# Value columns in another order, so that a unit of the attention's output and each output weight piece are one load

## The chip, the cores and the metric

One core of one Trainium2 chip runs the whole program. The metric is device time in microseconds (us), the median of several executions. Engines: PE is the matmul engine (PEld its weight loads), DVE the vector engine, ACT the scalar engine, POOL is GpSimd, and SP issues nearly all DMAs. A core has 16 DMA engines, which share the packets of a DMA between them.

## The reference

The input x has 2048 tokens of 640 values. The core of what is computed:

```python
xn  = layernorm(x)
q, k, v = split(xn @ wqkv)             # 32 heads of 20 values
s   = q @ k.T * 20 ** -0.5, only where 0 <= i - j < 256
a   = (softmax(s) @ v).reshape(2048, 640) @ wo
g   = silu(relu(xn @ w1 + b1) ** 2 @ w2 + b2)    # 1536 hidden values
out = x + a * g
```

## The kernel before, in words

All matmuls run on values split into a high and a low part, three products (high by high, high by low, low by high) for each, so a sum over 640 inputs takes 5 chunks x 3 = 15 matmuls.

**Start (L138 to L410).** x is loaded, normalised and transposed; the first q and k columns and all values are computed. The value weights come as five pieces `wvr` of 128 x 640 (L293). `wjobs` (L294) holds a triple of high, low and raw for each, and `split_w` (L187 to L189) works through it: ACT copies the high part, POOL subtracts for the low one. `v_part` (L231 to L233) multiplies with both. The order of the 640 columns in the pieces is the order in which values lie from there on: in v, in the attention's output and in the rows of `wo` that belong to it.

**Main part.** 16 pairs of heads by 16 tiles of 128 tokens are worked through in steps: scores, softmax, probabilities times values (L561, `ops`). PE's time between these is filled by a generator, `filler()`, with q and k groups for later pairs and the MLP (`hps`, `yps`, L473). A planner's clock, which counts estimated costs of PE's work, decides when each piece of work of another engine is written into the program: `later(wait, fn)` (L597) puts a task off until the clock has moved by `wait`. Engines and queues then work strictly in the order in which the program was written. Weights come through `piece` and `piece_pair` (L795 to L827): one load into one of three raw buffers `wraw`, a high part by ACT, a low part by DVE.

**The attention's output.** For a pair of heads and a group of 4 tiles, ACT copies `ops` into `osb` and SP stores it to `o_d[g]` (L568, issued at L588), in DRAM, as 128 rows of 256 tokens. Row 64h + 32e + d holds value d (0 to 19) of head h of the pair and tile parity e; row 20 holds the softmax's sum.

**The last stage.** It has 8 units u of 256 tokens, two for each of the four stores' groups g.
- `invert` (L1074 to L1087) loads a group's 64 rows of sums twice (L1081, `rec<-o`), after a planned wait FETCH takes the reciprocal on DVE (L1084) and stores it (L1085).
- `load(u)` (L1117 to L1131) brings a unit into `ob`: partition 32k + head, 5 chunks c of 256 tokens, where chunk c of block k is value 4c + k. These are four DMAs of 32 x 5 x 256 (L1126). A fifth, `sums` (L1127), reads the unit's 32 rows of reciprocals four times, once for each block k. For unit 0 alone, the planned wait BRING puts off what follows.
- `turn_out` (L1135 to L1151): DVE multiplies ob by sums in two cuts (L1145), ACT makes the high part `oT` (L1146), DVE the low one (L1149).
- `queue_wo` (L1161 to L1170) queues five output weight pieces of 128 rows, row 32k + head of piece c being the row of wo for value 4c + k of that head: four DMAs of 32 x 640 each (L1169, L798 to L801).
- `out_filler` (L1172 to L1218): for each unit 2 tiles x 2 halves of 15 matmuls (`wops`, L627), evacuation by DVE (L1209), the addition of x on POOL (L1215), a store of the tile. Around them it issues the loads of x (`xres`, L1115), of the MLP's results (`yq`, `yk`, L1104), and the next units.

`late()` (L933) calls load(0), load(1) and load(2) during the last groups of the MLP, whose evacuation on DVE is L1013 (`ysb`, from the bank `yps` and the earlier half `yin`). SP's DMAs use eight semaphores in turn, so that a DMA isn't issued before the one eight ahead of it has landed.

Of the kernel before, what the change touches and what calls it, by code (L numbers as in the profile page):

```python
# [19 lines left out]
H = 32  # L20
DH = 20
# [5 lines left out]
VW = DH + 1  # L27
# [22 lines left out]
SETTLE = 0.45  # L50
LEAD = 0.15
FETCH = 8.0
BRING = 8.0
SOON = 0.25
PATIENCE = 0.5

# [1 line left out]
def f32(ap):  # L58
    return ap.bitcast(F32)
# [3 lines left out]
def attn_mlp_kernel(ctx: ExitStack, tc, x, wqkv, wo, w1, b1, w2, b2, out):  # L63
    nc = tc.nc
# [25 lines left out]
    o_d = [dram.tile([NP, P, MT], F32, name=f"o_{g}") for g in range(NB)]  # L90
# [47 lines left out]
    with tc.tile_pool(name="ph1v", bufs=2) as p1v, tc.tile_pool(name="ph1", bufs=2) as p1, tc.tile_pool(name="ph1x", bufs=4) as p1b, tc.tile_pool(name="ph1w", bufs=1) as p1w, tc.tile_pool(name="ph1t", bufs=2, space=PSUM) as p1t:  # L138
# [9 lines left out]
        wv = [p1w.tile([P, KC, D], F32R, name=f"wv{p}") for p in range(2)]  # L148
# [119 lines left out]
        with tc.manual_schedule(engines={E_.PE, E_.Activation, E_.DVE, E_.Pool, E_.SP}):  # L268
# [15 lines left out]
            wjobs = []  # L284
# [6 lines left out]
            wvr = [wvt[c // 3][:, c % 3 * D:(c % 3 + 1) * D] for c in range(KC)]  # L291
            for c in range(KC):
                nc.sync.dma_start(wvr[c], wqkv[c * P:(c + 1) * P, 2 * D:3 * D])  # L293
                wjobs.append((wv[0][:, c, :], wv[1][:, c, :], wvr[c]))  # L294

            def root(t):
                nc.scalar.activation(rstd[:, t:t + 1], mv[:, t, 1:2], AF.Sqrt, bias=eps)
# [195 lines left out]
    def max_rows(p, g, tps):  # L493
        i = p % 2

        def one(j):
            r = slice(j * HP, (j + 1) * HP)
            nc.tensor.transpose(tps[:HP, j, 3 * P:3 * P + HP], mts[g % 2][r, :], ident[r, r])
        both(lambda: one(0), lambda: one(1), COST[P])

        def rest():
            row = at2.tile([8, P], F32, tag="row", bufs=1, name="row")
            mrow = at2.tile([8, 2, P], F32R, tag="mrow", bufs=1, name="mrow")
            nc.scalar.activation(row.rearrange("m (j n) -> m j n", j=2), tps[:8, :, 3 * P:3 * P + HP], AF.Copy, scale=-1.0)  # L504
            nc.scalar.activation(mrow[:, 0, :], row, AF.Copy)
            nc.gpsimd.tensor_sub(mrow[:, 1, :], row, f32(mrow[:, 0, :]))
            for a in range(2):
                nc.sync.dma_start(f32(qs[i])[KR + a:KR + a + HP + 1:HP, g * BT:(g + 1) * BT].rearrange("h (q n) -> h q n", q=4), f32(mrow)[:, a, :])
        return rest
# [3 lines left out]
    def pair_tile():  # L513
        return ptp.tile([P, 2, BT], F32, tag="st", name="stps")
# [25 lines left out]
    def burst_at(p, kb):  # L540
        return next((ts for ts in bursts(p) if ts[-1] == kb), None)
# [57 lines left out]
    def later(wait, fn):  # L599
        tasks.append((clock[0] + wait, len(tasks), fn))  # L600
# [177 lines left out]
    def subtract(tag, jobs):  # L778
        left = [len(jobs)]

        def put_off(k, job):
            def go():
                if item in lows:
                    lows.remove(item)
                    job()
                    left[0] -= 1
                    if not left[0]:
                        held[0] -= 1
            item = (tag, go)
            lows.append(item)  # L790
            later(1.9 + 0.7 * k, go)
        for k, job in enumerate(jobs):
            put_off(k, job)

    def piece(tag, src, go):  # L795
        def start():
            raw = wgt.tile([P, FHALF], F32, tag="wraw", bufs=RAW, name="raw")[:, :RAWN[tag[0]]]
            if isinstance(src, list):  # L798
                for k, rows in enumerate(src):
                    nc.sync.dma_start(raw[32 * k:32 * k + H], rows)  # L800
                return lambda tag: go(tag, raw)  # L801
            if len(src.shape) == 3:
                raw = raw.rearrange("p (c n) -> p c n", n=src.shape[-1])
            nc.sync.dma_start(raw, src)
            return lambda tag: go(tag, raw)
        queue.append((tag, start))
# [16 lines left out]
    def piece_pair(tag, hi, lo, src):  # L823
        def go(tag, raw):
            nc.scalar.activation(hi(), raw, AF.Copy)
            subtract(tag, [lambda: nc.vector.tensor_sub(lo(), raw, f32(hi()))])
        piece(tag, src, go)  # L827

    def lazy(make):
        got = []  # L830

        def get():
            if not got:
                got.append(make())
            return got[0]
        return get
# [42 lines left out]
    def filler():  # L879
# [53 lines left out]
        def late():  # L933
            j = lates[0]
            lates[0] += 1
            if j >= 3:
                load(0)
            if j >= 5:
                load(1)
            if j >= 7:  # L940
                load(2)

        for n, (hf, b) in enumerate(blocks):
# [6 lines left out]
            if n == last:  # L950
                wo_part = queue_wo()
                shut.add("o")
# [164 lines left out]
    def load(u):  # L1117
        if u in ld or u >= 2 * NB or recs.get(u // 2, 0) is not None:
            return
        if u % 2 == 0:  # L1120
            obs[u // 2] = bigp.tile([P, KC * BT], F32, tag="big", name=f"ob_{u // 2}")
        ob = obs[u // 2][:, u % 2 * 2 * D:(u % 2 + 1) * 2 * D].rearrange("p (c n) -> p c n", c=KC)
        sums = at2.tile([P, MT if u // 2 % 3 == 0 else BT], F32, tag=("sums", "relu", "sq")[u // 2 % 3], name="sums")[:, :MT]
        rows = o_d[u // 2].rearrange("p (h r) n -> (p h) r n", h=2)[:, 32 * (u % 2):32 * (u % 2) + VW]
        for k in range(4):
            nc.sync.dma_start(ob[32 * k:32 * k + H], rows[:, k:DH:4])  # L1126
        nc.sync.dma_start(sums, rec_d[u // 2][u % 2].unsqueeze(0).to_broadcast([4, H, MT]))  # L1127
        ld[u] = (ob, sums)
        if not u:
            for part in range(2):  # L1130
                later(BRING + 2.0 * part, lambda part=part: turn_out(0, part))  # L1131

    obs, oT, turned_out, shone = {}, {}, set(), set()

    def turn_out(u, part):  # L1135
        if (u, part) in turned_out or u not in ld:
            return
        turned_out.add((u, part))
        ob, sums = ld[u]
        cuts = (slice(0, 2), slice(2, KC))  # L1140
        if not part:
            big = bigp.tile([P, KC * BT], F32R, tag="big", name=f"oT_{u}")
            oT[u] = big.rearrange("p (s c n) -> p s c n", s=2, c=KC)
            for cs in cuts:
                nc.vector.tensor_mul(ob[:, cs], ob[:, cs], sums.unsqueeze(1).to_broadcast([P, cs.stop - cs.start, MT]))  # L1145
                nc.scalar.activation(oT[u][:, 0, cs], ob[:, cs], AF.Copy)  # L1146
        else:
            for cs in cuts:
                nc.vector.tensor_sub(oT[u][:, 1, cs], ob[:, cs], f32(oT[u][:, 0, cs]))  # L1149
            if whole[0]:  # L1150
                silu(u)  # L1151
# [9 lines left out]
    def queue_wo():  # L1161
        wob = lazy(lambda: [bigp.tile([P, KC * BT], F32R, tag="big", name=f"wo{j}") for j in range(2)])
        wo4 = lazy(lambda: [wgt.tile([P, FHALF], F32R, tag="wraw", bufs=RAW, name=f"wo4{w}")[:, :D] for w in "hl"])

        def wo_part(p, c):
            return wob()[p][:, c * D:(c + 1) * D] if c < 4 else wo4()[p]

        for c in range(KC):
            piece_pair("o", lambda c=c: wo_part(0, c), lambda c=c: wo_part(1, c), [wo.rearrange("(h d) n -> d h n", d=DH)[4 * c + k] for k in range(4)])  # L1169
        return wo_part  # L1170

    def out_filler(wo_part):  # L1172
# [71 lines left out]
    with tc.manual_schedule(engines={E_.PE, E_.Activation, E_.DVE, E_.Pool, E_.SP}):  # L1244
# [7 lines left out]
        for s in range(steps):  # L1252
# [8 lines left out]
            if a:  # L1261
                p, q = a
# [12 lines left out]
            rows = None  # L1275
# [4 lines left out]
            if s % 4 == 0 and 0 < s <= NP * NT:  # L1280
                rows = max_rows((s - 1) // NT, (s - 1) % NT // 4, stp[0] if b else pair_tile())
# [11 lines left out]
            r = e and burst_at(*e)  # L1293
# [41 lines left out]
```

## Time and profile before

| | |
|---|---|
| time, median of 3 runs | 849.57 us (848.41 to 850.68) |
| the profiled execution | 851.8 us, its span 849.7 us |
| mean granted PE clock | 0.995 |
| PE / PEld busy | 836.9 / 787.0 us |
| DVE / ACT / POOL busy | 458.6 / 420.5 / 329.9 us |
| DMA | 166.42 MB in 94398 packets, mean 196 GB/s |

The profile is of one execution. Times in rows are us from the start of the span unless a column says ns; "x12" counts instructions in a row; a bracket at a row's end gives the idle time of the engine before it and what ended that. In rows of windows PEclk is the granted clock as a share of full speed, and DMA share the mean busy share of the 16 DMA engines. Line numbers are those of the kernel before.

### The profile page before, as it was taken

What the parts mean: (1) busy time and instruction counts of PE and PEld (TensorE: products, weight loads), DVE (VectorE), ACT (ScalarE), POOL (GpSimd) and SP (SyncE); (2) the same over time, 40 slices, a digit from 0 to 9 for tenths busy, and PEclk for the clock granted to TensorE, in tenths of its full rate; (3) what the DMA queues carried; (4) which work ended last, traced back from release to release, by engine and by line L of the source; (5) the groups of instructions that cost most, each with busy time, mean ns of one, the idle gap of its engine ahead of it and who ended that gap; (6) DMA issues with size and microseconds to landing.
All of it is one profiled execution on the core that took longest, in us unless ns stands there. A gap on an engine that the chain in (4) does not pass through costs nothing.

```text
span 849.7 us, 25547 instructions
## 1 busy us (share of the span) xinstructions
PE 836.9 (98%) x10176; PEld 787.0 (93%) x10176; DVE 458.6 (54%) x1370; ACT 420.5 (49%) x792; POOL 329.9 (39%) x652
## 2 busy tenths in 40 slices
PE   8999999999999999999999999999999999989997
PEld 8999999988888999999999999899999999979997
DVE  7643126666577645455455476654455455345653
ACT  5232104555566754754754765745745736742321
POOL 5010002434334543553543644534533634532443
PEclk9999999999999999999999999999999999999999
DMA  7998488879989555364365264485285374376994
GB/s 245 284 389 336 161 207 259 256 249 273 300 268 302 128 182 156 84 200 132 78 214 166 77 179 136 128 266 154 63 269 135 110 223 120 102 171 180 274 231 150
DMA packets 94398, 166.42 MB, mean 196 GB/s; under 512 B 10952, under 2 KB 43848, under 8 KB 93256
## 3 DMA queue, kind: packets, MB, share of 16 engines
q1 hardware_dynamic: 94120, 164.64, 64.4%
q8 instruction: 80, 1.31, 0.7%
q14 instruction: 38, 0.31, 0.1%
q10 hardware_dynamic: 160, 0.16, 0.1%
HBM read 93.66 MB, written 70.52 MB: 193 GB/s over the span
## 4 chain that ended last, share of the span: by engine, by line
PE 87%; DMA 6%; DVE 2%; issue 2%; ACT 1%; SPq 1%; POOL 0%; DVEq 0%; ACTq 0%; POOLq 0%
PE yps L473 20%; PE hps L473 19%; PE qkps L473 14%; PE ops L561 10%; PE vps L233 8%; PE stps L523 5%; PE sps L483 4%; DMA ob<-o 4%; PE qkps L210 3%; PE wops L627 2%; DMA sums<-rec 1%; DMA yk<-y 1%; PE tps L177 1%; DMA o<-osb 1%; SPq L1126 0%
## 5 line engine op out<-in xcount | busy, mean ns | idle before, releaser
L491 DVE CUSTOM_DVE_ANT_0 junk<-sps,mask 128x384 bf16<-128x384 f32 (+2 forms) x512 | 272.1, 532 | 257.8 <-PE sps L483 86.8
L529 ACT ACTIVATE p<-stps 128x768 f32<-128x768 f32 (+2 forms) x256 | 197.4, 771 | 248.3 <-PE stps L523 203.0
L530 POOL TENSOR_SCALAR_AFFINE_SELECT p<-p 128x256 f32<-128x256 f32 x256 | 109.9, 429 | 326.1 <-ACT p L529 318.2
L473 PE MATMUL yps<-w,hh 64*128 64x320 f32 x1536 | 228.5, 312 | 4.2 <-DVE ysb L1013 3.4
L473 PE MATMUL hps<-xb,w 64*128 64x256 f32 (+1 forms) x2100 | 211.9, 304 | 0.0
L473 PEld LDWEIGHTS hps<-xb,w 64*128 64x128 f32 x2100 | 194.5, 187 | 3.8 <-issue 2.7
L473 PEld LDWEIGHTS yps<-w,hh 64*128 64x128 f32 x1536 | 187.0, 187 | 7.8 <-DVE ysb L1013 4.4
L473 PE MATMUL yps<-w,hl 64*128 64x320 f32 x768 | 177.8, 311 | 0.0
L483 PE MATMUL sps<-ks,qs 60*128 60x384 f32 (+2 forms) x512 | 131.5, 335 | 0.6 <-DVE mt L491 0.5
L523 PE MATMUL stps<-qs,ks 62*128 62x384 f32 (+2 forms) x512 | 126.3, 333 | 0.3 <-ACT row L504 0.2
L473 PEld LDWEIGHTS yps<-w,hl 64*128 64x128 f32 x768 | 120.4, 187 | 1.1 <-issue 1.0
L473 PE MATMUL qkps<-xT,wgkh 64*128 64x512 f32 x320 | 100.5, 394 | 0.0
L473 PE MATMUL qkps<-xT,wgqh 64*128 64x512 f32 x320 | 98.6, 392 | 0.0
L532 POOL TENSOR_SCALAR_AFFINE_SELECT p<-p 128x256 f32<-128x256 f32 x224 | 95.9, 428 | 0.0
L561 PE MATMUL ops<-p,vp 128*21 128x128 f32 (+1 forms) x2128 | 86.9, 311 | 0.0
L483 PEld LDWEIGHTS sps<-ks,qs 60*128 60x128 f32 x512 | 81.9, 185 | 4.4 <-DVE mt L491 2.2
L561 PEld LDWEIGHTS ops<-p,vp 128*21 128x21 f32 x2128 | 63.8, 100 | 21.2 <-issue 6.1
L523 PEld LDWEIGHTS stps<-qs,ks 62*128 62x128 f32 x512 | 80.7, 187 | 1.2 <-ACT row L504 0.6
L233 PE MATMUL vps<-wv,xT 128*128 128x320 f32 x480 | 71.5, 308 | 0.0
L233 PEld LDWEIGHTS vps<-wv,xT 128*128 128x128 f32 x480 | 70.5, 188 | 0.1
L983 POOL TENSOR_TENSOR hl<-sq,hh 128x512 fp32r<-128x512 f32 x48 | 62.2, 1295 | 16.4 <-ACT sq L982 16.2
L627 PE MATMUL wops<-wo,oT 128*128 128x320 f32 x384 | 62.2, 310 | 0.2 <-DVE res L1209 0.2
(104 smaller groups left out, 1160.1 us busy)
## 6 DMA issues: line engine op xcount, KB each, us to landing
ks<-k_d SPq DMA_DIRECT2D x64, 240.0 KB
qs<-q_d SPq DMA_DIRECT2D x64, 240.0 KB
xb<-xs SPq DMA_DIRECT2D x60, 256.0 KB
xs<-xT SPq DMA_DIRECT2D x8, 1280.0 KB
k_d<-shm SPq DMA_DIRECT2D x19, 512.0 KB
q_d<-shm SPq DMA_DIRECT2D x19, 512.0 KB
y<-ysb SPq DMA_DIRECT2D x28, 320.0 KB
o<-osb SPq DMA_DIRECT2D x64, 128.0 KB
```

The source lines that it names most:

```text
L210: nc.tensor.matmul(ps, wt[:, c, :], xT[part][b][:, c * BT + t0:c * BT + t0 + n], start=m == 1, stop=m == 3 * KC)
L233: nc.tensor.matmul(ps, xT[xp][b][:, c * BT + t * P: c * BT + (t + 1) * P], wv[wp][:, c, nh * HALF:(nh + 1) * HALF], start=first and m == 0 ...
L473: return nc.tensor.matmul(out, a[r], b_[r], skip_group_check=True, **kw)
L483: nc.tensor.matmul(ss[hh][:, :nk], qs[i][o, q * P:(q + 1) * P], ks[i][o, k0 * P:k0 * P + nk], start=True, stop=True)
L491: nc.vector.tensor_tensor_reduce(out=junk[:, :nk], in0=ss[hh][:, :nk], in1=mask[:, 3 * P - nk:], scale=1.0, scalar=-3.0e38, op0=ALU.add, o ...
L523: nc.tensor.matmul(tps[:, hh, :n], ks[i][o, kb * P:(kb + 1) * P], qs[i][o, kb * P:kb * P + n], start=True, stop=True)
L529: nc.scalar.activation(p32[:, :, :n], tps[:, :, :n], AF.Exp, scale=SCALE)
L530: nc.gpsimd.affine_select(p32[:, :, 0:P], p32[:, :, 0:P], pattern=[[0, 2], [1, P]], compare_op=ALU.is_ge, fill=0.0, base=0, channel_multip ...
L532: nc.gpsimd.affine_select(p32[:, :, 2 * P:], p32[:, :, 2 * P:], pattern=[[0, 2], [-1, P]], compare_op=ALU.is_gt, fill=0.0, base=0, channel ...
L561: nc.tensor.matmul(ot[r0:r0 + VW, c0:c0 + len(part), :], vps[p][:, kb // 4, kb % 4, hh, :], pt[:, hh, :].rearrange("p (t n) -> p t n", n=P ...
L627: nc.tensor.matmul(ps, a, b_, start=j == 0, stop=j == n - 1)
L983: nc.gpsimd.tensor_sub(hh[1][:, :BT], sq, f32(hh[0]))
```

## The change

The value columns get another order, the unit loads and the output weight pieces become one DMA each, and BRING goes from 8 to 9.

```diff
-BRING = 8.0
+BRING = 9.0
...
-                wjobs.append((wv[0][:, c, :], wv[1][:, c, :], wvr[c]))
+                wjobs.append((*(w[:, c, :].rearrange("p (h k c) -> p h k c", h=H, k=4) for w in wv), wvr[c].rearrange("p (h c k) -> p h k c", h=H, k=4)))
...
-            if isinstance(src, list):
-                for k, rows in enumerate(src):
-                    nc.sync.dma_start(raw[32 * k:32 * k + H], rows)
+            if tag[0] == "o":
+                nc.sync.dma_start(raw, src)
                 return lambda tag: go(tag, raw)
...
-        rows = o_d[u // 2].rearrange("p (h r) n -> (p h) r n", h=2)[:, 32 * (u % 2):32 * (u % 2) + VW]
-        for k in range(4):
-            nc.sync.dma_start(ob[32 * k:32 * k + H], rows[:, k:DH:4])
+        rows = o_d[u // 2].rearrange("p (h r) n -> (p h) r n", h=2)[:, 32 * (u % 2):32 * (u % 2) + DH]
+        nc.sync.dma_start(ob.rearrange("p c n -> p (c n)"), rows.rearrange("h (k c) n -> k h (c n)", k=4))
         nc.sync.dma_start(sums, rec_d[u // 2][u % 2].unsqueeze(0).to_broadcast([4, H, MT]))
...
-            piece_pair("o", ..., [wo.rearrange("(h d) n -> d h n", d=DH)[4 * c + k] for k in range(4)])
+            piece_pair("o", ..., wo.rearrange("(h d) n -> d h n", d=DH)[4 * c:4 * c + 4])
```

Within each head, value 4c + k now stands at place 5k + c instead of 4c + k. The splits of the value weights do this: their outputs are written in the order of memory, and their inputs read with a step of four elements (16 bytes) in runs of five. In `o_d`, the five rows that one partition of `ob` needs are then neighbours, 5 KB in one piece, where they were five pieces of 1 KB. The unit's load is one DMA whose source is walked as 4 blocks k, 32 heads, 1280 values, into 128 partitions; a weight piece is one DMA whose source is walked as 4, 32, 640 values. The load of `sums` is as before. In the changed kernel, the lines after the removed ones have numbers lower by 1 or 2.

On SP, around unit 0's load, the rows were these (a number at the end of a name tells buffers apart; o_85 and o_86 are the groups 0 and 1):

```order
L800 DMA raw<-in_A_wo_dram 32x640 x8
L1085 DMA rec_1359<-rec 128x128
L588 DMA o_86<-osb 128x256
L930 DMA yin<-y_83 128x640
L1081 DMA rec<-o_86 64x1x128 x2
L1126 DMA ob_13901<-o_85 32x5x256 x4
L1127 DMA sums<-rec_1359 128x1x256
L1126 DMA ob_13901<-o_85 32x5x256 x4
L1127 DMA sums<-rec_1359 128x1x256
L930 DMA yin<-y_83 128x640
```

and are now:

```order
L799 DMA raw<-in_A_wo_dram 128x1x640 x2
L1084 DMA rec_1359<-rec 128x128
L588 DMA o_86<-osb 128x256
L929 DMA yin<-y_83 128x640
L1080 DMA rec<-o_86 64x1x128 x2
L1124 DMA ob_13886<-o_85 128x1x1280
L1125 DMA sums<-rec_1359 128x1x256
L1124 DMA ob_13886<-o_85 128x1x1280
L1125 DMA sums<-rec_1359 128x1x256
L929 DMA yin<-y_83 128x640
```

Their sequence is the same; eight issues of weights became two, and four of a unit became one. The rest of SP's list differs in the same way alone.

On DVE, at the end of the MLP, the rows were these (ob are units 0 and 1, ysb the MLP's evacuation, oT the low part):

```order
L826 TENSOR_TENSOR wo4l<-raw,wo4h 128x640
L1084 RECIPROCAL rec<-rec 128x128
L1145 TENSOR_TENSOR ob_13901<-ob_13901,sums 128x512
L1145 TENSOR_TENSOR ob_13901<-ob_13901,sums 128x768
L1013 TENSOR_TENSOR ysb<-yps,yin 128x320
L1149 TENSOR_TENSOR oT_14055<-ob_13901,oT_14055 128x512
L1149 TENSOR_TENSOR oT_14055<-ob_13901,oT_14055 128x768
L1013 TENSOR_TENSOR ysb<-yps,yin 128x320 x3
```

and are now:

```order
L825 TENSOR_TENSOR wo4l<-raw,wo4h 128x640
L1083 RECIPROCAL rec<-rec 128x128
L1012 TENSOR_TENSOR ysb<-yps,yin 128x320
L1143 TENSOR_TENSOR ob_13886<-ob_13886,sums 128x512
L1143 TENSOR_TENSOR ob_13886<-ob_13886,sums 128x768
L1147 TENSOR_TENSOR oT_14059<-ob_13886,oT_14059 128x512
L1147 TENSOR_TENSOR oT_14059<-ob_13886,oT_14059 128x768
L1012 TENSOR_TENSOR ysb<-yps,yin 128x320 x3
```

One evacuation has moved ahead of unit 0's two multiplications. PE's list is unchanged.

More of the change, by code (lines that the diff above doesn't have):

```diff
@@ L1168, in queue_wo @@
         for c in range(KC):
-            piece_pair("o", lambda c=c: wo_part(0, c), lambda c=c: wo_part(1, c), [wo.rearrange("(h d) n -> d h n", d=DH)[4 * c + k] for k in range(4)])
+            piece_pair("o", lambda c=c: wo_part(0, c), lambda c=c: wo_part(1, c), wo.rearrange("(h d) n -> d h n", d=DH)[4 * c:4 * c + 4])
         return wo_part
```

## The prediction

> **What bounds the kernel now.** The page comes first: the span, TensorE's busy time, and the chain that ended last.
>
> ```profile
> span 849.7 us, 25547 instructions
> PE 836.9 (98%) x10176; PEld 787.0 (93%) x10176; DVE 458.6 (54%) x1370; ACT 420.5 (49%) x792; POOL 329.9 (39%) x652
> PE 87%; DMA 6%; DVE 2%; issue 2%; ACT 1%; SPq 1%; POOL 0%; DVEq 0%; ACTq 0%; POOLq 0%
> ```
>
> The profiled execution took 851.8 us, 2.1 outside its span; the median of three runs is 849.57. I work on the span and add its difference to the median. PE is the bound, and the chain's DMA share is the loads that the change rewrites. So I read PE's waits from 740 us to the end (columns: total, times, longest), then PE's and VectorE's rows there.
>
> ```profile
> PE yps L473 <- DVE ysb L1013: 3.4, 1, 3.4
> ```
> ```profile
> 754.02 0.95 DVE L1084 RECIPROCAL rec<-rec 128x128 f32<-128x128 f32 x1
> 760.71 1.56 DVE L1145 TENSOR_TENSOR ob<-ob,sums 128x512 f32<-128x512 f32 x2 [5.74 <-DMA ob<-o]
> 762.19 0.48 DVE L1013 TENSOR_TENSOR ysb<-yps,yin 128x320 f32<-128x320 f32 x1
> ```
> ```profile
> 762.73 0.90 PE L473 MATMUL yps<-w,hh 64*128 64x320 f32 x4 [3.40 <-DVE ysb L1013]
> 771.79 1.01 PE L627 MATMUL wops<-wo,oT 128*128 128x320 f32 x5
> ```
>
> DVE waits 5.74 us for unit 0's load, multiplies, and only then evacuates the MLP's bank for which PE has stood 3.40 us. The windows show what follows (columns: length, busy time and count of PE, PEld, DVE, ACT, POOL, then granted clock, DMA share, GB/s).
>
> ```profile
> core 0: us, PE busy (x) PEld busy (x) DVE busy (x) ACT busy (x) POOL busy (x), PEclk, DMA share, GB/s
> 759.33:762.73 3.40, 0.01 (x2) 0.01 (x2) 2.02 (x4) 1.06 (x2) 0.00 (x0) 0.89 0.93 190
> 762.73:768.40 5.67, 5.67 (x39) 5.67 (x40) 1.90 (x3) 3.34 (x5) 0.92 (x1) 0.50 0.18 53
> 768.40:771.79 3.39, 3.39 (x23) 3.20 (x21) 0.49 (x1) 0.00 (x0) 0.00 (x0) 0.94 0.86 204
> 757.00:759.00 2.00, 2.00 (x31) 2.00 (x28) 0.00 (x0) 0.00 (x0) 0.00 (x0) 1.00 1.10 201
> 763.40:764.10 0.70, 0.70 (x8) 0.70 (x8) 0.70 (x1) 0.68 (x2) 0.61 (x1) 0.50 0.27 89
> 790.00:794.00 4.00, 4.00 (x29) 4.00 (x29) 2.64 (x4) 0.63 (x1) 2.02 (x2) 1.00 1.03 405
> ```
>
> After the stop the clock is 0.50 for 5.67 us, which loses half of them. One stop costs 3.40 + 2.8 = 6.2 us; that is all there is to gain here, since PE waits for nothing else that is long.
>
> **The order: a gain of up to 6.2 us.** With the planner's due time (BRING) one later, the evacuation stands ahead of the two multiplications on DVE. It then waits only for its own matmuls, which were over by 759.33, and for the reciprocal behind 754.02. The stop goes, and PE would reach the output matmuls at 771.79 - 6.2 = 765.6. What is late next is unit 0 itself, so the loads decide.
>
> **The loads.** Before, a unit is four DMAs of 32 x 5 x 256 and its sums are one, which reads 32 rows four times.
>
> ```profile
> 750.43 1.21 SPq L1081 DMA_DIRECT2D rec<-o  x2
> 751.73 2.64 SPq L1126 DMA_DIRECT2D ob<-o  x4
> 754.41 0.58 SPq L1127 DMA_DIRECT2D sums<-rec  x1
> 755.03 1.91 SPq L1126 DMA_DIRECT2D ob<-o  x4
> 756.98 0.56 SPq L1127 DMA_DIRECT2D sums<-rec  x1
> 757.63 0.42 SPq L930 DMA_DIRECT2D yin<-y  x1
> ```
>
> The two kinds move differently. While the four-piece loads run (757 to 759) the DMA engines are all busy, 1.10. From 763.40 to 764.10 the share is 0.27, about 4 of 16 engines, and the packets there are these:
>
> ```profile
> DMA packets 61, 0.06 MB, mean 89 GB/s; under 512 B 0, under 2 KB 61, under 8 KB 61
> q1 hardware_dynamic: 61, 0.06, 26.9%
> ```
>
> All are of 1 KB, so the longer rows of yin are over and the last of the queue, the second sums, runs alone: on about four engines. Its source walks an outermost dimension of 4, then 32 rows, into 128 partitions. The new unit load has exactly that form (4, 32, runs of 5 KB), and so have the new output weight pieces (4, 32, 640 values). I take it that they too run on four engines. The Trainium skill, "DMA: Bandwidth & Descriptors", says so in "Rules for kernel authors": an outermost dimension of fewer than 16, a leading broadcast for instance, confines a DMA to that many engines. By that rule, with which the share of 0.27 agrees, the sum below stands as it is; without it the sum would be that of the first rival.
>
> Prices per engine: the sums moved 89 GB/s on 0.27 x 16 engines, 20.6 GB/s each; rows of 2.5 KB moved 405 GB/s at 1.03 x 16, 24.6 each. A unit is 128 x 5 KB = 655 KB, 164 KB on each of four: 6.66 us at 24.6, 7.95 at 20.6. I take 24.6, since 5 KB is nearer to the long rows. Its sums are 33 KB on each: 1.59. Together 8.25 us a unit. A transfer of 128 x 2560 B on all 16 takes each of the four 0.83, a weight piece now 3.33.
>
> Every other DMA has a share on these four engines, in order, so I add up their work from unit 0's load to unit 7's sums. The new order of SP has 8 units x 8.25 = 66.0; 28 transfers of 2560 B rows (inputs, earlier results, outputs) x 0.83 = 23.2; two stores of o, four loads and two stores of reciprocals, about 1.8 by bytes. That is 91.0. PE needs the following for a unit:
>
> ```profile
> 797.76 1.92 PE L627 MATMUL wops<-wo,oT 128*128 128x320 f32 x12
> 799.96 1.92 PE L627 MATMUL wops<-wo,oT 128*128 128x320 f32 x12
> ```
>
> 2.20 us a group, four groups, 8.8 a unit, 70.4 for eight. So the loads, with 91.0, become the bound by some 20 us. Two stops come on top. SP issues in order and waits for each store of o before it reads the sums from it:
>
> ```profile
> 748.61 0.38 SPq L588 DMA_DIRECT2D o<-osb  x1
> SPq L1081 <- DMA o<-osb: 11.4, 4, 5.2
> ```
>
> Such a store, queued behind unit loads, lands when the four engines run dry; then SP issues the two sum loads (1.21) and the unit, whose first bytes come about 1.8 later, as long as the store took from 748.61 to the next issue at 750.43. That is 3.1 of idle engines, twice: 6.2. Sum 97.2.
>
> **Where it starts.** Weight pieces 4 and 5 go out just ahead:
>
> ```profile
> 744.44 3.60 SPq L800 DMA_DIRECT2D raw<-in_A_wo_dram  x8
> ```
>
> Fewer issues, 3.60 to about 0.9, but 2 x 3.33 on the four engines, from about 746.1 (issue plus 1.7). Store o_86 behind them lands at about 753.6 and not by 750.43; two sum loads 1.2, unit 0 issued at 754.8, moving from 756.4. Its sums land at 764.7, its oT is there at 766.9: about where PE arrives, so unit 0 loses little. The last sums land at 756.4 + 97.2 = 853.6. The three earlier pieces have time and cost PE nothing.
>
> The rest is the end, with its rows (first those of the unit's tile: ns least/median/most, first and last start):
>
> ```profile
> L1145 DVE TENSOR_TENSOR ob<-ob,sums x16: 681/821/1634, 760.7 to 831.9; 128x512 f32<-128x512 f32 x8, 128x768 f32<-128x768 f32 x8
> L1146 ACT ACTIVATE oT<-ob x16: 631/739/850, 761.4 to 832.9; 128x512 fp32r<-128x512 f32 x8, 128x768 fp32r<-128x768 f32 x8
> L1149 DVE TENSOR_TENSOR oT<-ob,oT x16: 676/816/1648, 762.6 to 833.8; 128x512 fp32r<-128x512 f32 x8, 128x768 fp32r<-128x768 f32 x8
> ```
> ```profile
> 844.72 0.31 PE L627 MATMUL wops<-wo4h,oT 128*128 128x320 f32 x1
> ```
>
> Multiply, high and low of unit 7's first pieces (0.7 + 0.65 + 0.75, about 2.2 with the hand-overs) bring 855.8; 8.8 of matmuls 864.6; from the last matmul's end (845.0) to the span's end 4.7: 869.3. That is 19.6 over 849.7, and 849.57 + 19.6 = **869.2**. Two units lie 8.25 + 4 x 0.83 = 11.6 apart on the engines, so PE stands 2.8 at most between late units, less than the 3.40 after which the clock halved; I add nothing for the clock, and 2.8 for the last unit as upper end.
>
> **The permuted value weights.** The splits now read every fourth value (16 bytes apart) within a head.
>
> ```profile
> 13.92 0.74 ACT L188 ACTIVATE wv<-wvr 128x640 fp32r<-128x640 f32 x1
> 15.27 7.68 POOL L189 TENSOR_TENSOR wv<-wvr,wv 128x640 fp32r<-128x640 f32 x5
> 20.27 8.96 PE L233 MATMUL vps<-wv,xT 128*128 128x320 f32 x60
> ```
>
> PE needs the fifth low part at about 23.8 (24 of 60 matmuls of 0.149); POOL delivers at 22.95, 0.85 ahead. No row has such a step, so the price lies between nothing and a doubling of 1.57: five of them 7.8 late, 7.0 of it on PE. Below nothing I exclude: the work is the same. I take nothing, since the nearest row is the contiguous one and the two operands keep their shape; the rest is a rival. ACT's copy may double from 0.74 and is still quicker than POOL's 1.57. The order of value columns changes no later step's size.
>
> **Rivals.** *The load spreads over 16 engines, because of its 128 partitions.* Then only the order counts: 849.57 - 6.2 = 843.4, faster. For it: the stop is real and the bytes are no more. Against: the 0.27 of the sums. It decides near eight engines: a unit is then 3.33 + 1.59, and eight of them with the 25.0 and 6.2 of the rest are 70.6, level with PE's 70.4. Chance 0.13.
>
> *GpSimd's strided reads are slow.* If each takes half as long again, five are 3.9 late, 3.1 of it on PE: 872.3 beside the forecast, 846.5 beside the first rival. The Trainium skill, "GPSIMD Engine Reference", "Performance pitfalls for Q7 kernels", states such a price for reads more than 8 bytes apart; no run here shows it. It needs only a slip of 0.85 us to reach PE. Chance 0.3 within either case.
>
> *Four engines, but less is lost:* if no engine runs dry at the two stops and the weights come on time, 869.2 - 6.2 - 2.7 = 860.3; with the transfers between the units overlapping better, some us less. At 20.6 GB/s it is 8 x 1.3 = 10.3 more, 879.5; with slow reads and the halved clock 885. These are the forecast's ends.
>
> **Numbers.** Loads on four engines 0.84, loads spread 0.13 (with or without the slow reads), something in between 0.03. The range takes the first case's ends, 856 to 885, and leaves the second outside. A measurement of this kernel tells about 0.3% from no change; faster 0.14, within it 0.02, slower 0.84.
>
> **What would show it.** On four engines: DMA share near 0.25 for some 6 us after each unit's issue, DVE's multiplications waiting for ob or sums, PE waiting for oT from unit 2 or 3 on, units 11 to 15 us apart at the end, no 3.40 before the last MLP matmuls. Wrong would be: a share near 1 in unit loads, with PE's waits gone. Slow reads show in the duration of POOL's five subtractions and a wait of PE near 23 us.

## The result, and the profile after

The changed kernel took 889.22 us (median of 4 runs, 888.67 to 891.34) beside 848.99 us for the kernel before (4 runs): a ratio of 1.0475, 95% interval 1.0451 to 1.0499. The prediction was 869.2 with a range of 856 to 885: the sign was right, but the time lies above the range, and the loss of 40.2 us is twice the forecast's 19.6.

The profiled execution has a span of 887.3 us. First the page of the changed kernel:

```profile
span 887.3 us, 25475 instructions
PE 848.8 (96%) x10176; PEld 796.3 (90%) x10176; DVE 455.4 (51%) x1370; ACT 423.9 (48%) x792; POOL 331.2 (37%) x652
PE 81%; DMA 10%; SPq 2%; DVE 2%; issue 2%; ACT 1%; POOL 1%; DVEq 0%; POOLq 0%
```

DMA's share of the chain went from 6% to 10%. Next the waits from 740 us to the end (columns: total, times, longest):

```profile
DVE ob L1143 <- DMA sums<-rec: 49.6, 6, 12.5
PE wops L627 <- DVE res L1207: 25.5, 9, 7.2
```

PE no longer waits for the MLP's evacuation, where it had stood 3.40 us; it waits 25.5 us in the output matmuls for banks that DVE evacuates late, because DVE's queue stands at the multiplication of the next unit, which waits for its load. These are the eight multiplications, one row for each unit, in order:

```profile
767.51 1.56 DVE L1143 TENSOR_TENSOR ob<-ob,sums 128x512 f32<-128x512 f32 x2 [9.66 <-DMA sums<-rec]
776.94 1.55 DVE L1143 TENSOR_TENSOR ob<-ob,sums 128x512 f32<-128x512 f32 x2
794.09 1.56 DVE L1143 TENSOR_TENSOR ob<-ob,sums 128x512 f32<-128x512 f32 x2 [10.72 <-DMA rec<-rec]
815.92 1.56 DVE L1143 TENSOR_TENSOR ob<-ob,sums 128x512 f32<-128x512 f32 x2 [12.50 <-DMA sums<-rec]
831.39 1.56 DVE L1143 TENSOR_TENSOR ob<-ob,sums 128x512 f32<-128x512 f32 x2 [8.55 <-DMA sums<-rec]
843.89 1.56 DVE L1143 TENSOR_TENSOR ob<-ob,sums 128x512 f32<-128x512 f32 x2 [5.58 <-DMA sums<-rec]
855.27 1.56 DVE L1143 TENSOR_TENSOR ob<-ob,sums 128x512 f32<-128x512 f32 x2 [6.07 <-DMA sums<-rec]
867.79 1.56 DVE L1143 TENSOR_TENSOR ob<-ob,sums 128x512 f32<-128x512 f32 x2 [7.21 <-DMA sums<-rec]
```

Their distances are 9.4, 17.2, 21.8, 15.5, 12.5, 11.4 and 12.5 us, where PE needs 8.8 for a unit. The windows of the changed kernel (columns as in the prediction) show how the loads move:

```profile
757.00:761.00 4.00, 4.00 (x58) 4.00 (x56) 0.84 (x2) 0.39 (x1) 0.41 (x1) 1.00 0.24 82
785.00:790.00 5.00, 3.93 (x27) 3.67 (x26) 0.00 (x0) 0.00 (x0) 0.00 (x0) 1.00 1.06 173
770.00:775.00 5.00, 5.00 (x50) 3.52 (x51) 1.34 (x2) 2.61 (x3) 0.00 (x0) 0.54 0.25 94
```

With a unit's load alone (757 to 761, 770 to 775) the share is 0.24 and 0.25: four engines of sixteen. The Trainium skill, "DMA: Bandwidth & Descriptors", "Rules for kernel authors", has it that an outermost dimension of c below 16 keeps a DMA on at most c engines; the trace agrees. From 785 to 790, with the five loads of x beside unit 2's, all engines count as busy and move only 173 GB/s, less than half of what a window of before showed at nearly the same share (405 at 1.03).

### The profile page after: what moved, and what is told of

The parts are those of the page before. It is cut to its first block, busy times and chain, and to the rows that moved or that the text cites. A ratio compares the mean times of both kernels' runs of the same rounds, so it can differ in the third digit from the quotient of the medians.

```text
span 887.3 us, 25475 instructions
## 1 busy us (share of the span) xinstructions
PE 848.8 (96%) x10176; PEld 796.3 (90%) x10176; DVE 455.4 (51%) x1370; ACT 423.9 (48%) x792; POOL 331.2 (37%) x652
## 4 chain that ended last, share of the span: by engine, by line
PE 81%; DMA 10%; SPq 2%; DVE 2%; issue 2%; ACT 1%; POOL 1%; DVEq 0%; POOLq 0%
PE yps L473 19%; PE hps L473 19%; PE qkps L473 13%; PE ops L561 9%; PE vps L233 8%; PE stps L523 5%; PE sps L483 4%; DMA sums<-rec 3%; DMA xres<-in_A_x_dram 3%; PE qkps L210 2%; DMA yin<-y 2%; PE wops L627 1%; DMA o<-osb 1%; POOL wv L189 1%; PE tps L177 1%
## 5 line engine op out<-in xcount | busy, mean ns | idle before, releaser
L473 PE MATMUL yps<-w,hh 64*128 64x320 f32 x1536 | 226.2, 310 | 0.8 <-ACT relu L977 0.8
L473 PEld LDWEIGHTS yps<-w,hh 64*128 64x128 f32 x1536 | 184.3, 185 | 4.1 <-ACT relu L977 1.6
L473 PE MATMUL yps<-w,hl 64*128 64x320 f32 x768 | 175.3, 308 | 0.0
L473 PEld LDWEIGHTS yps<-w,hl 64*128 64x128 f32 x768 | 117.3, 185 | 1.1 <-issue 1.0
L627 PE MATMUL wops<-wo,oT 128*128 128x320 f32 x384 | 73.4, 347 | 29.3 <-DVE res L1207 25.5
L627 PEld LDWEIGHTS wops<-wo,oT 128*128 128x128 f32 x384 | 67.3, 219 | 32.7 <-DVE res L1207 24.4
L561 PEld LDWEIGHTS ops<-p,vp 128*21 128x21 f32 x2128 | 64.3, 101 | 21.8 <-issue 6.8
```

The source lines that it names most:

```text
L473: return nc.tensor.matmul(out, a[r], b_[r], skip_group_check=True, **kw)
L561: nc.tensor.matmul(ot[r0:r0 + VW, c0:c0 + len(part), :], vps[p][:, kb // 4, kb % 4, hh, :], pt[:, hh, :].rearrange("p (t n) -> p t n", n=P ...
L627: nc.tensor.matmul(ps, a, b_, start=j == 0, stop=j == n - 1)
```

## The experiments

The theory: what is slow are the loads that walk an outermost dimension of 4. The rivals: the order that BRING 9 makes, the splits with a step, one DMA a unit as such.

**The unit load on sixteen engines, by four DMAs.**

```diff
-nc.sync.dma_start(ob.rearrange("p c n -> p (c n)"), rows.rearrange("h (k c) n -> k h (c n)", k=4))
+for k in range(4):
+    nc.sync.dma_start(ob[32 * k:32 * k + H].rearrange("p c n -> p (c n)"), rows[:, KC * k:KC * k + KC].rearrange("h c n -> h (c n)"))
```

> The changed kernel with the unit load alone as four DMAs again, one for each block of 32 partitions, with its runs of 5 KB kept. Theory (the unit load of one DMA walks an outermost dimension of 4 and so moves on four DMA engines): a unit's load runs on all sixteen, DMA share near 1 while it does, no wait of PE in the output matmuls, no stop before the last MLP matmuls; about 845 us, within 842 to 850. Rival (the loss comes from elsewhere: weight pieces, sums, or the order that BRING 9 gives): it stays above 870.

853.22 us, ratio 1.0051 (1.0036 to 1.0066): 36 of the 40 us are gone, so the unit load's form carries most of the loss. The last 4 are not: PE still waits 6.6 us in the output matmuls, and with the weight pieces as in the changed kernel unit 0's load is issued as late as there (754.82). The window of this run in which the first two units load:

```profile
756.00:761.00 5.00, 5.00 (x72) 5.00 (x71) 1.30 (x2) 0.41 (x2) 0.63 (x2) 1.00 0.97 228
```

All engines are busy, yet at 228 GB/s. The forecast of 845, within 842 to 850, missed that.

**One DMA each, with 32 heads outermost.** Partition 4 x head + k takes the place of 32k + head.

```diff
-rows.rearrange("h (k c) n -> k h (c n)", k=4)
+rows.rearrange("h (k c) n -> h k (c n)", k=4)
...
-rec_d[u // 2][u % 2].unsqueeze(0).to_broadcast([4, H, MT])
+rec_d[u // 2][u % 2].unsqueeze(1).to_broadcast([H, 4, MT])
...
-wo.rearrange("(h d) n -> d h n", d=DH)[4 * c:4 * c + 4]
+wo.rearrange("(h d) n -> h d n", d=DH)[:, 4 * c:4 * c + 4]
```

> The changed kernel with partitions 4 x head + k in place of 32 x k + head, so that the unit load, the sums and the weight pieces are one DMA each as now, of the same bytes, and each walks 32 heads outermost. Theory (it is the outermost dimension of 4): all three run on sixteen engines, 843 to 846 us, and no share near 0.25 is left in the last stage. Rival (one DMA for a unit is itself late, since nothing of it can be used before the whole has landed, whatever engines it runs on): above 855.

843.4 us, 0.9944 (0.9929 to 0.9959). The same bytes in as many DMAs, 46 us quicker: one DMA a unit is no loss, the outermost 4 is. Windows of this run, while units 0 and 1, unit 2 and unit 4 load:

```profile
753.00:756.00 3.00, 3.00 (x64) 2.60 (x58) 1.21 (x2) 0.99 (x3) 1.17 (x3) 1.00 0.91 320
764.00:766.00 2.00, 2.00 (x26) 1.62 (x29) 1.25 (x3) 0.07 (x1) 0.00 (x0) 1.00 1.00 374
785.00:788.00 3.00, 3.00 (x23) 3.00 (x22) 3.00 (x5) 1.77 (x3) 1.70 (x2) 1.00 1.03 408
```

**The same without the splits' step.** With value 5k + c in chunk c, a partition's five values are neighbours in their own order, and no column moves.

```diff
-wjobs.append((*(w[:, c, :].rearrange("p (h k c) -> p h k c", h=H, k=4) for w in wv), wvr[c].rearrange("p (h c k) -> p h k c", h=H, k=4)))
+wjobs.append((wv[0][:, c, :], wv[1][:, c, :], wvr[c]))
...
-wo.rearrange("(h d) n -> h d n", d=DH)[:, 4 * c:4 * c + 4]
+wo.rearrange("(p c) n -> c p n", c=KC)[c]
```

> As the run with partitions 4 x head + k, but with value 5k + c in chunk c, so that the value columns stay in their own order and the splits of the value weights read without a step. Theory (the strided splits cost PE 0.8 us near 23 us and little more): 0 to 1 us below the run with the permuted columns. Rival (the strided splits cost the start several us, hidden in the changed kernel's total): 3 us or more below it.

842.17 us, 0.9925 (0.9909 to 0.9942): 1.2 us below the run before it, a little over the expected 1, and the best of all here. Its splits beside those of the changed kernel, first the run's, then the changed kernel's (ns: least, median, most):

```profile
L188 ACT ACTIVATE wv<-wvr x5: 734/740/743, 12.5 to 16.2; 128x640 fp32r<-128x640 f32 x5
L189 POOL TENSOR_TENSOR wv<-wvr,wv x5: 1582/1593/1601, 13.9 to 20.0; 128x640 fp32r<-128x640 f32 x5
```
```profile
L188 ACT ACTIVATE wv<-wvr x5: 1407/1426/1452, 12.6 to 18.6; 128x640 fp32r<-128x640 f32 x5
L189 POOL TENSOR_TENSOR wv<-wvr,wv x5: 1864/1927/1944, 14.1 to 21.7; 128x640 fp32r<-128x640 f32 x5
```

**The order alone.** `BRING = 9.0` in the kernel before.

> The kernel before with BRING 9 alone. Theory (the moved evacuation ends the 3.40 us stop and the halved clock behind it, and nothing is late next): 842.8 to 845 us, no wait of PE above 1 us after 740 us. Rival (unit 0 is then itself late, or the order costs something): within 1.5 us of the kernel before or above it.

848.98 us, 1.0000 (0.9990 to 1.0011): nothing. PE's waits of this run from 740 us on hold one row of weight:

```profile
PE wops L627 <- DVE res L1209: 3.3, 1, 3.3
```

The 3.40 us stop is gone and one of 3.3 has come, near 801 us: the evacuation that PE then needs stands in DVE's queue behind unit 4's multiplication, which starts at 799.55, when its load is there. The stop moved to the next unit that is late.

**Order beside quick loads.** `BRING = 8.0` in the best run.

> The run with value 5k + c in chunk c (sixteen engines, splits without a step), with BRING 8. Theory (unit 0 is now here early enough that the multiplications hardly wait, so that the order is worth little by then): 842 to 844.5 us, a stop of less than 1.5 us before the last MLP matmuls. Rival (the order is worth the 6.2 us of the prediction whatever the loads): 847 to 849.

842.53 us, 0.9914 (0.9898 to 0.9931), as good as with 9: unit 0 starts its multiplications at 755.94 and PE does not wait. So the 6.2 us were to be had by loads that come early, and by the order not at all.

**Order beside slow loads.** `BRING = 8.0` in the changed kernel.

> The changed kernel with BRING 8, so that the MLP's evacuation stands behind unit 0's multiplications again. Theory (the loads on four engines set the end, and PE's time before unit 2 or 3 doesn't count): PE stops some 9 us before the last MLP matmuls and the end stays within 2 us of the changed kernel, 887 to 891. Rival (PE's own work still sets a part of the end): 895 or more.

890.52 us, 1.0475 (1.0451 to 1.0500). PE's waits of this run:

```profile
PE wops L627 <- DVE res L1207: 21.7, 8, 7.1
PE yps L473 <- DVE ysb L1012: 10.9, 1, 10.9
```

PE stands 10.9 us more before the last MLP matmuls, and the end hardly moves: PE does not set it, the loads do.

**The sums alone on sixteen engines.** Four DMAs `sums[32 * k:32 * k + H] <- rec_d[u // 2][u % 2]` in place of the one.

> The changed kernel with the sums alone as four DMAs of 32 rows, on sixteen engines. Theory (what is bound are the first four DMA engines, so every byte taken off them counts): eight times 1.6 us less, about 876 us. Rival (the time goes into the unit loads' own wait, and the sums behind them are hidden): 887 to 890.

886.99 us, 1.0443 (1.0422 to 1.0465): 2.2 us and not 12.7. That is the rival's number, and the sum of bytes on four engines is refuted as a plain sum. SP's rows and waits of this run point to where the freed time went:

```profile
758.46 8.35 SPq L1126 DMA_DIRECT2D sums<-rec  x4
...
779.03 11.73 SPq L1114 DMA_DIRECT2D xres<-in_A_x_dram  x5
```
```profile
SPq L1114 <- DMA ob<-o: 9.5, 1, 9.5
SPq L1126 <- DMA ob<-o: 6.6, 1, 6.6
```

Three more DMAs for each unit fill the eight places that SP has for DMAs under way, so that the last of these issues waits until a unit's load has landed: four issues take 8.35 us, five 11.73 (in the changed kernel 6.67).

**Weight pieces on sixteen engines.** Four DMAs `raw[32 * k:32 * k + H] <- src[k]` again.

> The changed kernel with the output weight pieces as four DMAs of 32 rows again. Theory (pieces 4 and 5 hold the store of group 1 back on the four engines by some 3 us and so move all unit loads): unit 0's load is issued 2 to 3 us earlier, 886 to 887.5 us. Rival (that delay is absorbed by the waits behind it): within 1 us of the changed kernel.

883.12 us, 1.0406 (1.0380 to 1.0432): 6 us less. Unit 0's load is issued at 750.23 (755.08 in the changed kernel), and its multiplications start 4.7 us earlier:

```profile
762.78 1.56 DVE L1144 TENSOR_TENSOR ob<-ob,sums 128x512 f32<-128x512 f32 x2 [5.30 <-DMA sums<-rec]
```

The direction was expected, the size was not: the forecast was 886 to 887.5.

**All of them as four DMAs.** Unit loads, sums and pieces as in the three runs above.

> The changed kernel with unit loads, sums and weight pieces each as four DMAs of 32 partitions, so that all of them run on sixteen engines and only the order of the values, the runs of 5 KB and BRING 9 are left of the change. Theory A (only the count of engines matters): 843 to 844.5 us, as with partitions 4 x head + k. Theory B (a DMA into 32 neighbouring partitions moves at half rate, some 200 to 230 GB/s as the unit loads did in the run with four loads a unit, against 340 to 430 with partitions 4 x head + k): slower windows in unit loads, a wait of PE or two in the output matmuls, 845 to 850.

845.97 us, 0.9965 (0.9952 to 0.9977): in theory B's range, 2.6 us above the single DMAs with heads outermost. PE's waits of this run, and the window in which unit 2 loads:

```profile
PE wops L627 <- DVE res L1210: 3.1, 4, 2.1
```
```profile
766.00:769.00 3.00, 3.00 (x51) 2.60 (x52) 1.92 (x3) 2.54 (x5) 0.00 (x0) 1.00 0.91 229
```

In this order of undoing, the 46 us between the changed kernel and the run with heads outermost are 36 for the unit loads, 7.2 for sums and weight pieces, and 2.6 for what is left between four DMAs into 32 partitions each and one.

**Four DMAs, each into every fourth partition.** In the run with heads outermost, `ob[k:P:4] <- rows[:, KC * k:KC * k + KC]` for each k.

> The kernel with partitions 4 x head + k, the unit load as four DMAs, each into every fourth partition. Its reads are those of the run with four loads a unit (32 heads, 5 KB, 64 KB apart), its writes are spread over all 128 partitions. If the half rate comes from writing 32 neighbouring partitions: unit loads at 340 to 430 GB/s, 843 to 844 us. If it comes from the reads 64 KB apart, or from four DMAs in place of one: about 220 GB/s.

843.74 us, 0.9938 (0.9923 to 0.9953). Windows of this run, while units 0 to 2 load:

```profile
753.00:756.00 3.00, 3.00 (x61) 2.42 (x60) 1.61 (x3) 1.17 (x3) 0.79 (x2) 1.00 0.74 235
765.00:768.00 3.00, 3.00 (x50) 2.37 (x50) 2.82 (x4) 1.49 (x3) 0.00 (x0) 1.00 0.84 247
```

The rate, 235 to 247, is nearer to the 220 that would have spoken for the reads or the four DMAs than to the 340 expected, so the rate alone doesn't decide. But the engines are not full here: SP takes 3.78 us over the four issues of unit 0 and 2.46 over those of unit 2. Per busy engine it is 235 / (16 x 0.74) = 19.8 and 247 / (16 x 0.84) = 18.4 GB/s, against 228 / (16 x 0.97) = 14.7 into 32 neighbouring partitions and 320 / (16 x 0.91) = 22.0 with one DMA. The single packets of 5 KB in the traces tell more: their median is 196 ns in each of the eight units here, as with one DMA, and 318 to 395 ns in the units of the run with four loads into 32 neighbouring partitions each. With the same reads, it is the writes into 32 neighbouring partitions that slow. (Sums and weight pieces are single DMAs here, so the 2.2 us to the run before are not the unit loads' alone.) The Trainium skill, "SBUF — State Buffer", "Door 1: The DMA port swizzle", states that partitions 0 to 31 reach 8 of the 16 ports, about 218 GB/s; the 228 of the run with four loads a unit and the 201 of the kernel before's unit loads lie close to it on either side.

**Without the loads of x.** `xts[t] = None`, and the last addition takes the gate `ybt[t]` in place of x, so that the output lacks x.

> The changed kernel without the sixteen loads of x for the last addition (the gated value is added to itself; x is left out of the output). Theory C (a unit load on four engines is slowed to half where a load on sixteen engines moves beside it: the 5 KB packets of units 2 and 3 took twice the time while x was loaded): unit 2's load is as quick as unit 0's, some 7 us where it took 13; 13.3 us of work taken off the four engines and 6 to 9 us of slowing, 866 to 870 us. Rival D (5 KB packets on the four engines have one price, near 20 GB/s): 13.3 us less alone, about 876.

871.42 us, 1.0256 (1.0237 to 1.0274): 17.8 less, between the two and closer to theory C's 866 to 870. The interval (869.3 to 872.5) leaves D's 876 out, but the four runs spread from 869.49 to 876.51, and the profiled one is the slowest: its unit 0 is multiplied 5.1 us later than in the changed kernel (772.56), so distances tell more than times here. Unit 2's load tells most, since the loads of x stand behind it in the queue and can't delay it but by moving beside it: by D it would come no earlier. In this run the multiplications of units 1 and 2 are 13.4 us apart, 17.2 in the changed kernel:

```profile
782.01 1.55 DVE L1142 TENSOR_TENSOR ob<-ob,sums 128x512 f32<-128x512 f32 x2
...
795.36 1.56 DVE L1142 TENSOR_TENSOR ob<-ob,sums 128x512 f32<-128x512 f32 x2 [6.31 <-DMA sums<-rec]
```

and the window 788 to 793 of this run, in its load, shows four engines at the rate of an undisturbed unit, 88 / (16 x 0.25) = 22 GB/s each:

```profile
788.00:793.00 5.00, 5.00 (x36) 5.00 (x36) 1.05 (x3) 0.00 (x0) 2.55 (x3) 1.00 0.25 88
```

From its first to its last packet, unit 2's load took 9.1 us in place of 12.9. Unit 3's, beside which earlier results of the MLP are loaded in both runs, took 12.0 and 11.5: it gained nothing.

**Heads 66 KB apart.** `o_d` with 66 rows a head, `o_d = dram.tile([NP, 2, HP + 2, MT])`, and two stores in place of one.

> The changed kernel with 66 rows for a head in the DRAM copy of o in place of 64, so that heads lie 66 KB and not 64 KB apart; each store of o becomes two of 64 rows. If the 5 KB packets of units 2 and 3 take double the time because reads 64 KB apart meet in one place of the memory: they fall from about 400 to about 200 ns, and the time to 875 to 882 us. If the slowing comes from the writes or from the number of engines: no change in them, 887 to 893 us.

892.19 us, 1.0507 (1.0485 to 1.0529): no gain. Where x is loaded beside unit 2, this run moves 216 GB/s at a share of 1.07:

```profile
785.00:790.00 5.00, 5.00 (x36) 5.00 (x35) 0.49 (x2) 0.00 (x0) 0.00 (x0) 1.00 1.07 216
```

That is not the 405 of the window of before; the run with BRING 8, its heads still 64 KB apart, has 208 in the same window. The distance of the reads is not the cause.

## Why the prediction was wrong

By its own steps:

- **Four engines, so slower**: right. The share, the waits and the runs with four loads a unit and with heads outermost show it.
- **Start at 756.4**: right by the row (issue at 755.08, forecast 754.8). But the cost of the weight pieces was put at 2.7 us; undoing them gave 6.
- **The price of a unit, 6.66 us at 24.6 GB/s an engine whatever moves beside it**: this is the step that failed. Unit 0 moved at 82 GB/s where it was alone, 655 / 82 = 8.0 us, the upper end (7.95) that I had put aside; and units 2 and 3, with sixteen-engine loads beside them, took longer still. From first to last packet, the eight unit loads of the changed kernel took 9.1, 7.8, 12.9, 11.5, 9.2, 8.4, 8.2 and 9.0 us. From unit 0's to unit 7's multiplication I had 853.6 - 764.7 = 88.9 us; it was 867.79 - 767.51 = 100.3. By the same sum (8.25, the transfers between, 3.1 for a stop) units 2 and 3 were to follow 12.6 and 16.7 us after the unit before; they followed 17.2 and 21.8 us after it, and that is nearly all that was missed between the units. Units 5 to 7, at 12.5, 11.4 and 12.5, are close to the 11.6 of the forecast, but in part by luck: their loads took 8.2 to 9.0 us, and the sums and transfers between them cost less than the sum gives them, as the run with the sums alone also shows (2.2 us for 12.7).
- **PE free for unit 7, and nothing for the clock**: wrong. The forecast lets unit 7's matmuls begin 2.2 us after its multiplication starts. But PE still had the last of unit 6's four groups to do, whose bank DVE evacuated only behind that multiplication (867.79). DVE's evacuation, then PE's last group of unit 6, the first of unit 7, and the last matmul:

```profile
869.27 0.48 DVE L1207 TENSOR_TENSOR res<-wops,yq 128x320 f32<-128x320 f32 x1
869.81 3.28 PE L627 MATMUL wops<-wo,oT 128*128 128x320 f32 x12 [3.04 <-DVE res L1207]
873.65 1.92 PE L627 MATMUL wops<-wo,oT 128*128 128x320 f32 x12
882.30 0.31 PE L627 MATMUL wops<-wo4h,oT 128*128 128x320 f32 x1
```

  After the wait of 3.04 us the granted clock was 0.50 (871 to 873), and twelve matmuls took 3.28 us, not 1.92: the group took 3.8 in place of 2.2, and unit 7's own matmuls began 5.9 us after its multiplication. They took 9.0 us (873.65 to 882.6), as forecast (8.8).
- **The sum**: unit 0 later by 2.8 us, units 1 to 7 by 11.4, from unit 7's multiplication to its first matmul 3.7, its matmuls 0.2, the tail 0: before rounding 18.0, and 869.3 + 18.0 = 887.3, the span. So 14.2 of the 18.0 stand before unit 7's multiplication, in the loads, and 3.7 in the way that PE reached unit 7.
- **The strided splits at nothing**: nearly. POOL's rose from 1568 to 1927 ns, and PE waited 0.81 us near 23.6; by the two runs with heads outermost the step costs 1.2 us. The Trainium skill, "GPSIMD Engine Reference", "Performance pitfalls for Q7 kernels", gives half as much again for such reads; 23% was measured. ACT's copy, for which I had only a bound of double, nearly reached it (739 to 1426 ns) and hid.
- **The gain of 6.2 us from the order**: wrong in its cause. The rival's 843.4 came out to the digit with loads on sixteen engines, but by luck: the order alone brings 0.0 and with quick loads it is worth nothing. I had read "PE waits for nothing else that is long" as "nothing is late next"; unit 4 was.

What stays open is why a load on four engines slows when another moves beside it. That it does is shown at unit 2 by leaving x out; the distance of the reads is excluded. Both loads slow: from 785 to 790 us of the changed kernel, the median packet of unit 2 (5 KB) took 472 ns and that of x (2560 B) 252, where undisturbed ones took 200 and 102. Writes into few partitions are slow when sixteen engines make them, but whether that is what slows these four was not tried.

## What to carry to other kernels

Before several loads are made one, look at the outermost dimension of the new one: four blocks outermost cost 40 us here, the same bytes with 32 heads outermost gained 5.7. A rate from one window holds for what moved in that window; where a slow transfer meets others, price it with them beside it. And a wait that one reorders away is a gain only if the next late thing is known: here it was the next unit, 3.3 us in place of 3.4.

## What the runs showed of the hardware

- DMAs into 32 neighbouring partitions moved 14.7 GB/s per busy engine, into every fourth one 18.4 and 19.8, one DMA over all 128 partitions 22.0 and more; packets of 5 KB took 318 to 395 ns (medians of the units) in the first, 196 in the other two.
- A load of 655 KB on four engines took 7.8 us at best in the changed kernel, and 12.9 with a sixteen-engine load beside it.
- ACT's copy of 128 x 640 values took 1426 ns with reads 16 bytes apart, and 740 ns without; POOL's subtraction 1927 and 1593.
- Work taken off four overloaded DMA engines need not come back: sums worth 12.7 us gave 2.2, and SP's issues, held by eight DMAs in flight, grew longer.
